# A fused convolution, GELU and two-matmul kernel: first token blocks over two DMA rings, W_in in halves copied across in SBUF, last block stored group by group

## Chip, cores and metric

The kernel runs on one core of one Trainium2 chip. The metric is device time in microseconds (us). Before the change the median of the first four runs is 714.08 us (713.27 to 714.69). A profile's span is about 2 us shorter than the device time of the same run.

Names: PE is TensorE, PEld its weight loads, DVE VectorE, ACT ScalarE, POOL GpSimd, SP SyncE; SPq and ACTq are the DMA issues of SP and ScalarE. A "ring" is the queue of DMAs that one of them issues. "Landing" is when a DMA's semaphore reports it.

## The reference, cut to what matters

```python
w = softmax(weight)                    # 8 heads x 7 taps
# x: 8 x 4096 x 192; causal 7-tap convolution along the sequence, taps per head
out = einsum('hk,bskhg->bshg', w, x_unf)
x = out.reshape(32768, 192)
h = x @ w_in                           # 192 x 2048
g = 0.5 * h * (1.0 + erf(h / sqrt(2))) # exact GELU
return g @ w_out                       # 2048 x 192
```

## The kernel before

The tokens are two halves of 16384, one half on partitions 0 to 63 and the other on 64 to 127, so that two 64-row matmuls share the array. They are cut into 33 blocks per half: two of 256 tokens, then 31 of 512. For each block VectorE transposes and convolves (3 transposes, 21 tap operations), TensorE multiplies by W_in in slices (mm1), ScalarE applies Gelu, and TensorE multiplies by W_out (mm2) during mm1 of the next block. VectorE evicts the result in groups of 128 tokens of each half.

W_in is needed in bf16 on both halves of the partitions. GpSimd loads it with a cast: the first FC = 512 columns twice, once for each half; the other 1536 columns once, and SP then copies them from partitions 0-63 to 64-127 in SBUF.

```python
# GpSimd
g.wait_ge(S_XIN[0], 64)                       # x block 0 has landed
for hf in range(2):
    g.dma_start(win[half hf, columns 0:FC], w_in[..., 0:FC]).then_inc(S_WIN[0], 16)
halo(0)
g.wait_ge(S_XIN[1], 64)                       # x block 1 has landed
g.dma_start(win[half 0, FC:F], w_in[..., FC:F]).then_inc(S_WIN[1], 16)
g.dma_start(wout, w_out).then_inc(S_WOUT, 16)
for n in range(1, NB): halo(n)
# SP
load(0)                                       # 4 DMAs per block
sp.wait_ge(S_XIN[0], 64)
load(1)
sp.wait_ge(S_WIN[1], 16)
sp.dma_start(win[half 1, FC:F], win[half 0, FC:F]).then_inc(S_WIN[2], 16)
load(2)
for n in range(1, NB + 1):
    if n + 2 < NB: load(n + 2)
    store(n - 1)                              # waits for all groups of the block
# TensorE, ahead of mm1 of a block / of the first slice past column FC
t.wait_ge(S_CV, NCV * (n + 1))                # the block's convolution
t.wait_ge(S_WIN[1], 16); t.wait_ge(S_WIN[2], 16)
# ... (cut, in simplified notation)
```

## Time and profile before

| Read from | Before |
|---|---|
| span; TensorE busy | 711.7 us; 95% |
| x block 2 landed; VectorE's wait for it | 34.9; 9.06 us |
| TensorE starts block 2 | 50.66 |
| TensorE's last stretch ends (start of the last eviction) | 706.05 |
| last eviction's start to the end of the span | 5.65 us |

The first fence is the timeline of the kernel before. Columns: start, length (both us), engine, source line, operation, output<-input, count; in brackets how long the engine had been idle just before, and what ended that. A line can merge several instructions, with gaps between them.

```profile
...
0.82 7.07 SPq L434 DMA_DIRECT2D xin<-in_x_dram  x8
...
6.26 1.10 DVE L215 STREAM_TRANSPOSE xT<-xin 128x256 f32<-128x256 f32 x3 [0.74 <-DMA xin<-in_x_dram]
...
13.81 0.63 POOL L178 DMA_DIRECT2D win<-in_moe_w_in_dram  x1 [5.28 <-DMA xin<-in_x_dram]
...
16.44 2.74 PE L361 MATMUL hp<-xc,win 64*128 64x256 bf16 x24 [11.14 <-DVE xc L245]
...
20.10 0.70 SPq L482 DMA_DIRECT2D win<-win  x1
...
27.72 6.04 PE L361 MATMUL hp<-xc,win 64*128 64x256 bf16 x60 [8.54 <-DMA win<-win]
...
34.91 1.90 DVE L215 STREAM_TRANSPOSE xT<-xin 128x512 f32<-128x512 f32 x3 [9.06 <-DMA xin<-in_x_dram]
...
```

VectorE starts at 6.26, and waits 9.06 us for x block 2 at 34.91. TensorE waits 8.54 us for the SBUF copy (`win<-win`) at 27.72. Only one of these waits ends last. The next fence is the chain of waits of the same kernel, in order of time: start, length, and what the next step waited for.

```profile
...
7.46 6.07 DMA xin<-in_x_dram
...
13.81 6.27 DMA win<-in_moe_w_in_dram
20.10 0.70 SPq L482
...
23.82 11.07 DMA xin<-in_x_dram
...
50.66 1.47 PE hp L361 x6
...
```

It runs through x block 1, W_in, x block 2, its convolution and then TensorE's block 2. W_in is in it because SP waits for W_in to issue the copy (20.10), and issues x block 2 only behind that. TensorE's wait for the copy is not in it: TensorE, had it had the data, would have waited for the convolution anyway. From 50.66 the chain is TensorE's to the last eviction.

Why do the loads take until 34.9? This fence is the table of stretches (stretch and length in us; busy time and count of PE, PEld, DVE, ACT, POOL; granted TensorE clock; mean busy share of the 16 DMA engines; GB/s).

```profile
...
4.00:5.00 1.00, 1.00 (x6) 1.00 (x6) 0.00 (x0) 0.43 (x1) 0.00 (x0) 1.00 0.96 229
5.00:6.00 1.00, 0.30 (x2) 0.20 (x1) 0.18 (x1) 0.00 (x0) 0.00 (x0) 1.00 0.01 0
6.00:7.00 1.00, 0.00 (x0) 0.00 (x0) 0.74 (x3) 0.00 (x0) 0.54 (x1) 1.00 0.00 0
12.00:13.00 1.00, 0.00 (x0) 0.00 (x0) 1.00 (x3) 0.00 (x0) 0.00 (x0) 1.00 0.42 61
13.00:14.00 1.00, 0.00 (x0) 0.00 (x0) 1.00 (x4) 0.00 (x0) 0.19 (x1) 1.00 0.09 14
14.00:15.00 1.00, 0.00 (x0) 0.00 (x0) 1.00 (x3) 0.00 (x0) 1.00 (x2) 1.00 0.00 0
...
```

Twice the engines have next to nothing to do: each next load waits until the one before it has been reported as landed. And the same table at the start of block 2 shows the clock:

```profile
...
50.00:51.00 1.00, 0.34 (x2) 0.16 (x4) 1.00 (x3) 0.00 (x0) 0.00 (x0) 0.55 0.00 0
...
53.00:54.00 1.00, 1.00 (x15) 0.64 (x13) 0.96 (x2) 0.31 (x2) 0.69 (x2) 0.75 0.13 27
54.00:55.00 1.00, 1.00 (x21) 0.64 (x18) 1.00 (x4) 1.00 (x2) 0.32 (x1) 1.00 0.48 113
...
```

TensorE had been idle for 3.67 us before block 2 and starts it at half clock (0.55 in the first of these stretches), which lasts until about 53.5 (0.75 is the mean of a stretch half at each). A caution on this column: where the trace has no clock record it reads 1.00, and the first record stands at 19.37 here. So the 1.00 of the first stretches says nothing. The end of the timeline:

```profile
...
696.08 12.69 SPq L461 DMA_DIRECT2D out_dram<-osb  x8
...
706.05 0.56 DVE L254 COPY osb<-ob 128x384 f32<-128x384 f32 x1 [0.76 <-PE ob L393]
```

The last four of these eight stores (192 KB each, the whole last block) are issued only after the last eviction, from 706.6 on.

### The profile page before, as it was taken

Reading aid. Unit: us, or ns where it says so; the run is one execution under the profiler, and the core shown is the slowest. Engines: PE = TensorE matmul, PEld = TensorE weight load, DVE = VectorE, ACT = ScalarE, POOL = GpSimd, SP = SyncE. Lnnn points to the kernel's source line nnn. Section 1 sums busy time; section 2 is a strip of 40 time slices with the busy share of each in tenths; the row PEclk is TensorE's granted clock in tenths of the full one; section 3 lists DMA queues with packets and bytes.
Section 4 is the critical chain, followed back from the end, with each engine's and each line's share of the span. In section 5 each row is a group of like instructions: output and inputs, shape, how many; then the busy total and the mean of one; then the engine's idle time right before and its main releaser. Section 6 shows DMA issues by size and latency. Waiting matters only on the chain.

```text
span 711.7 us, 24838 instructions
## 1 busy us (share of the span) xinstructions
PE 677.3 (95%) x11366; PEld 511.9 (72%) x11366; DVE 563.4 (79%) x925; ACT 526.4 (74%) x516; POOL 37.4 (5%) x77
## 2 busy tenths in 40 slices
PE   1479999999999999999999999999999999999996
PEld 1366777777777777777777777777777777777776
DVE  6499898888889888889888888988888898888701
ACT  1459777777777777777777777777777777777770
POOL 3001000000000000000000000000000000000000
PEclk9799999999999999999999999999999999999999
DMA  6925455544455654345554434555444555543013
GB/s 129 214 57 119 101 134 135 129 104 92 91 122 134 134 122 100 86 97 134 134 134 110 99 84 111 134 134 128 106 95 91 120 134 134 127 96 86 9 44 91
DMA packets 20553, 78.92 MB, mean 111 GB/s; under 512 B 6496, under 2 KB 7904, under 8 KB 16480
## 3 DMA queue, kind: packets, MB, share of 16 engines
q1 hardware_dynamic: 17744, 75.56, 46.9%
q0 software_dynamic: 2688, 1.77, 1.9%
q8 instruction: 89, 1.46, 0.9%
q14 instruction: 16, 0.13, 0.1%
q10 hardware_dynamic: 16, 0.00, 0.0%
HBM read 53.33 MB, written 25.17 MB: 110 GB/s over the span
## 4 chain that ended last, share of the span: by engine, by line
PE 92%; DMA 4%; DVE 2%; SPq 1%; issue 0%
PE ob L393 47%; PE hp L361 45%; DMA xin<-in_x_dram 3%; DVE acc L245 1%; DMA win<-in_moe_w_in_dram 1%; SPq L434 1%; DVE acc L238 0%; DVE xT L215 0%; DVE xc L245 0%; SPq L482 0%; DVE osb L254 0%
## 5 line engine op out<-in xcount | busy, mean ns | idle before, releaser
L321 ACT ACTIVATE gT<-hp 128x1024 bf16<-128x1024 f32 x512 | 523.5, 1024 | 167.9 <-PE hp L361 167.9
L361 PE MATMUL hp<-xc,win 64*128 64x512 bf16 (+1 forms) x3168 | 425.5, 374 | 24.8 <-DVE xc L245 14.8
L393 PEld LDWEIGHTS ob<-wout,gT 64*128 64x128 bf16 x8192 | 364.4, 94 | 107.3 <-issue 0.5
L393 PE MATMUL ob<-wout,gT 64*128 64x192 bf16 x8192 | 426.5, 243 | 0.0
L245 DVE SCALAR_TENSOR_TENSOR acc<-xT,wcol,acc 128x512 f32<-128x512 f32 (+1 forms) x495 | 326.6, 720 | 0.0
L361 PEld LDWEIGHTS hp<-xc,win 64*128 64x128 bf16 x3168 | 159.2, 95 | 82.8 <-issue 26.1
L254 DVE COPY osb<-ob 128x384 f32<-128x384 f32 x128 | 69.9, 546 | 127.6 <-PE ob L393 127.6
L215 DVE STREAM_TRANSPOSE xT<-xin 128x512 f32<-128x512 f32 (+1 forms) x99 | 60.7, 664 | 9.8 <-DMA xin<-in_x_dram 9.8
L245 DVE SCALAR_TENSOR_TENSOR xc<-xT,wcol,acc 128x512 bf16<-128x512 f32 (+1 forms) x99 | 66.4, 718 | 0.0
L238 DVE TENSOR_SCALAR acc<-xT,wcol 128x512 f32<-128x512 f32 (+1 forms) x99 | 57.5, 632 | 1.2
L164 POOL COPY xT<-xT 128x558 f32<-128x558 f32 x33 | 21.6, 653 | 609.2 <-DVE xT L215 609.2
L155 POOL COPY xT<-xT 128x18 f32<-128x18 f32 x29 | 12.1, 419 | 0.0
L332 PE MATMUL ob<-wnm,sel 8*128 8x7 f32 x6 | 1.4, 354 | 3.9 <-DVE wnm L200 3.9
L332 PEld LDWEIGHTS ob<-wnm,sel 8*128 8x128 f32 x6 | 1.3, 320 | 3.9 <-issue 3.9
L298 ACT ACT_TABLE_LOAD x1 | 1.3, 1283 | 1.4 <-PEq L506 1.4
L192 DVE TENSOR_REDUCE wmx<-wsb 8x1 f32<-8x7 f32 x1 | 0.1, 149 | 2.2 <-DMA wsb<-in_weight_dram 2.2
L171 POOL DMA_DIRECT2D win<-in_moe_w_in_dram x2 | 1.4, 686 | 4.0 <-DMA xin<-in_x_dram 4.0
L204 DVE COPY wcol<-ob 128x21 f32<-128x21 f32 x1 | 0.2, 181 | 1.6 <-PE ob L332 1.6
L321 ACT ACT_TABLE_LOAD x1 | 1.3, 1283 | 0.0
L182 POOL DMA_DIRECT2D wout<-in_moe_w_out_dram x1 | 1.2, 1192 | 0.0
L178 POOL DMA_DIRECT2D win<-in_moe_w_in_dram x1 | 0.6, 632 | 5.3 <-DMA xin<-in_x_dram 5.3
L152 POOL MEMSET xT<- 128x18 f32 x4 | 0.8, 206 | 0.0
(12 smaller groups left out, 2.9 us busy)
## 6 DMA issues: line engine op xcount, KB each, us to landing
xin<-in_x_dram SPq DMA_DIRECT2D x124, 380.0 KB, 7.1
out_dram<-osb SPq DMA_DIRECT2D x124, 192.0 KB, 3.1
xin<-in_x_dram SPq DMA_DIRECT2D x8, 188.0 KB, 3.6
wout<-in_moe_w_out_dram POOLq DMA_DIRECT2D x1, 768.0 KB, 10.5
out_dram<-osb SPq DMA_DIRECT2D x16, 48.0 KB, 1.7
win<-in_moe_w_in_dram POOLq DMA_DIRECT2D x1, 576.0 KB, 6.3
win<-win SPq DMA_DIRECT2D x1, 576.0 KB, 7.5
win<-in_moe_w_in_dram POOLq DMA_DIRECT2D x2, 192.0 KB, 6.3
```

Of the source, the lines that this page charges most:

```text
L155: g.tensor_copy(dst, ap(xT[(n - 1) % 2], WS[n - 1] + 31, [[NP * XW, 128], [XW, NP], [32, HB]],),).then_inc(S_HALO)
L164: g.tensor_copy(ap(xT[n % 2], 1, [[NP * XW, 128], [XW, NP], [32, HB], [1, 31]]), ap(xT[n % 2], WS[n], [[NP * XW, 128], [XW, NP], [32, HB], ...
L171: g.dma_start(ap(win, 64 * hf * NP * F, [[NP * F, 64], [F, NP], [1, FC]]), ap(wint, 0, [[F, 64], [64 * F, NP], [1, FC]]),).then_inc(S_WIN[ ...
L215: v.transpose(ap(xT[n % 2], p * XW + HL, [[NP * XW, 128], [1, w]]), ap(xin[n % NX], 64 * p, [[TB // 32 * D, 128], [D, w // 32], [1, 32]],) ...
L238: ins = v.tensor_scalar(a, src, wk, None, ALU.mult)
L245: ins = v.scalar_tensor_tensor(dst, src, wk, a, op0=ALU.mult, op1=ALU.add)
L254: v.tensor_copy(ap(osb[m % 2], g * C, [[8 * C, 128], [4 * C, 2], [1, C]]), ap(ob[(G0[m] + g) % 2], 0, [[1024, 128], [512, 2], [1, C]]),).t ...
L321: a.activation(out=ap(gT[n % 2], i * c * 2 * w, dst), in_=ap(hp[u % 2], 0, src), func=AF.Gelu,).then_inc(S_GELU)
L332: ins = t.matmul(ob[0][:, p * KS : (p + 1) * KS], sel[:, p * 128 : (p + 1) * 128], wnm[:, :],)
L361: ins = t.matmul(hp[u % 2][:, hf * TB + cc * w : hf * TB + cc * w + w], win[r, p * F + f0 : p * F + f0 + 128], xc[n % 2][r, p * TB : p * T ...
L393: ins = t.matmul(ob[gg % 2][:, 512 * sub : 512 * sub + C], gT[m % 2][r, c0 : c0 + 128], wout[r, i * C : (i + 1) * C], start=(ph == 0 and i ...
L434: sp.dma_start(ap(xin[n % NX], 32 * q * (TB // 32 * D), [[TB // 32 * D, 32], [1, mb * D - 32]],), ap(xt, off, [[mb * D, 32], [1, mb * D - ...
```

## The change

Its intent: get the first blocks of x and W_in in sooner, and have less left to store after the last eviction. Blocks 0 and 1 of x are issued by SP and ScalarE, two DMAs of each block, without waiting for each other. W_in's loads wait for nothing; FC is 256; the other columns are loaded in two pieces, one to each half of the partitions, and an SBUF copy carries each across. The last block is stored group by group on both rings, for which its Gelu writes another token order.

```diff
-        FC = 512
+        FC = 256
+        FM = (FC + F) // 2
 # GpSimd
-            g.wait_ge(S_XIN[0], 64)
             for hf in range(2):
                 g.dma_start(... columns 0:FC ...).then_inc(S_WIN[0], 16)
-            halo(0)
-            g.wait_ge(S_XIN[1], 64)
-            g.dma_start(... half 0, FC:F ...).then_inc(S_WIN[1], 16)
+            for hf, c0, c1 in ((0, FC, FM), (1, FM, F)):
+                g.dma_start(... half hf, c0:c1 ...).then_inc(S_WIN[1], 16)
             g.dma_start(... wout ...)
-            for n in range(1, NB):
+            for n in range(NB):
                 halo(n)
 # ScalarE
-            a.dma_start(wsb[:, :], ...)
+            load(a, 0, (2, 3))
             a.wait_ge(S_PRO, 1); a.activation(... Exp ...)
+            load(a, 1, (2, 3))
 # ...
+            for g in range(NG[NB - 1]):
+                store_group(a, NB - 1, g, (2, 3))
 # SP
-            load(0)
-            sp.wait_ge(S_XIN[0], 64)
-            load(1)
-            sp.wait_ge(S_WIN[1], 16)
-            sp.dma_start(... half 1 <- half 0, FC:F ...).then_inc(S_WIN[2], 16)
-            load(2)
+            sp.dma_start(wsb[:, :], ...)
+            load(sp, 0, (0, 1))
+            load(sp, 1, (0, 1))
+            sp.wait_ge(S_WIN[1], 32)
+            for hf, c0, c1 in ((1, FC, FM), (0, FM, F)):
+                sp.dma_start(... half hf <- half 1 - hf, c0:c1 ...).then_inc(S_WIN[2], 16)
+            load(sp, 2)
 # ...
+            for g in range(NG[NB - 1]):
+                store_group(sp, NB - 1, g, (0, 1))
```
(cut: the store helpers and the semaphore counts)

More of the change, by code (lines that the diff above doesn't have):

```diff
@@ L58, in bass_lightweight_conv__then__act_gelu_exact_kernel @@
     G0 = [sum(NG[:n]) for n in range(NB + 1)]
+    PLAIN = [NCH[n] > 1 or n == NB - 1 for n in range(NB)]
     OUTS = []
     for n in range(NB):
-        OUTS.append((64 if NCH[n] == 1 else 128) + (OUTS[n - 2] if n >= 2 else 0))
+        OUTS.append((64 * NG[n] if PLAIN[n] else 64) + (OUTS[n - 2] if n >= 2 else 0))
     es = ExitStack()
@@ L118, in bass_lightweight_conv__then__act_gelu_exact_kernel, with load, store_group, store @@
         NCV = NP * KS
-        FC = 512
+        FC = 256
+        FM = (FC + F) // 2
+        def load(e, n, qs=(0, 1, 2, 3)):
+            mb = WS[n] // 32
+            if n >= NX:
+                e.wait_ge(S_TR, NP * (n - NX + 1))
+            for q in qs:
+                off = ((q // 2) * HALF + OFF[n]) * D + 32 * (q % 2)
+                e.dma_start(
+                    ap(
+                        xin[n % NX],
+                        32 * q * (TB // 32 * D),
+                        [[TB // 32 * D, 32], [1, mb * D - 32]],
+                    ),
+                    ap(xt, off, [[mb * D, 32], [1, mb * D - 32]]),
+                ).then_inc(S_XIN[n % NX], 16)
+        def store_group(e, m, g, qs=(0, 1, 2, 3)):
+            mb = WS[m] // 32
+            e.wait_ge(S_EV, G0[m] + g + 1)
+            for q in qs:
+                e.dma_start(
+                    ap(
+                        outt,
+                        (OFF[m] + 4 * g + q) * C,
+                        [[mb * C, 32], [HALF * C, 2], [1, C]],
+                    ),
+                    ap(
+                        osb[m % 2],
+                        32 * q * 8 * C + g * C,
+                        [[8 * C, 32], [4 * C, 2], [1, C]],
+                    ),
+                ).then_inc(S_OUT[m % 2], 16)
+        def store(e, m):
+            if PLAIN[m]:
+                for g in range(NG[m]):
+                    store_group(e, m, g)
+                return
+            j = NG[m]
+            mb = WS[m] // 32
+            e.wait_ge(S_EV, G0[m + 1])
+            for q in range(4):
+                e.dma_start(
+                    ap(
+                        outt,
+                        (OFF[m] + j * q) * C,
+                        [[mb * C, 32], [HALF * C, 2], [1, j * C]],
+                    ),
+                    ap(
+                        osb[m % 2],
+                        32 * q * 8 * C,
+                        [[8 * C, 32], [4 * C, 2], [1, j * C]],
+                    ),
+                ).then_inc(S_OUT[m % 2], 16)
         @block.gpsimd
@@ L174, in _ @@
                 ).then_inc(S_WIN[0], 16)
-            halo(0)
-            g.wait_ge(S_XIN[1], 64)
-            g.dma_start(
-                ap(win, FC, [[NP * F, 64], [F, NP], [1, F - FC]]),
-                ap(wint, FC, [[F, 64], [64 * F, NP], [1, F - FC]]),
-            ).then_inc(S_WIN[1], 16)
+            for hf, c0, c1 in ((0, FC, FM), (1, FM, F)):
+                g.dma_start(
+                    ap(win, 64 * hf * NP * F + c0, [[NP * F, 64], [F, NP], [1, c1 - c0]]),
+                    ap(wint, c0, [[F, 64], [64 * F, NP], [1, c1 - c0]]),
+                ).then_inc(S_WIN[1], 16)
             g.dma_start(
@@ L295, in _ @@
         def _(a):
-            a.dma_start(wsb[:, :], ap(wt, 0, [[KS, H], [1, KS]])).then_inc(S_WSB, 16)
+            load(a, 0, (2, 3))
             a.wait_ge(S_PRO, 1)
@@ L312, in _ @@
                         a.wait_ge(S_MM2, G0[n - 1])
-                    if c == 1:
+                    if not PLAIN[n]:
                         src = [[2 * TB, 128], [w // 4, 8], [32, w // 128], [1, 32]]
@@ L352, in mm1 @@
                 if seen[0] == 1 and 128 * (i + 1) * c > FC:
-                    t.wait_ge(S_WIN[1], 16)
-                    t.wait_ge(S_WIN[2], 16)
+                    t.wait_ge(S_WIN[1], 32)
+                    t.wait_ge(S_WIN[2], 32)
                     seen[0] = 2
@@ L427, in _ @@
         def _(sp):
-            def load(n):
-                mb = WS[n] // 32
-                if n >= NX:
-                    sp.wait_ge(S_TR, NP * (n - NX + 1))
-                for q in range(4):
-                    off = ((q // 2) * HALF + OFF[n]) * D + 32 * (q % 2)
-                    sp.dma_start(
-                        ap(
-                            xin[n % NX],
-                            32 * q * (TB // 32 * D),
-                            [[TB // 32 * D, 32], [1, mb * D - 32]],
-                        ),
-                        ap(xt, off, [[mb * D, 32], [1, mb * D - 32]]),
-                    ).then_inc(S_XIN[n % NX], 16)
@@ L443, in store @@
-            def store(m):
-                w = WS[m]
-                j = w // 128
-                mb = w // 32
-                sp.wait_ge(S_EV, G0[m + 1])
-                for q in range(4):
-                    if NCH[m] == 1:
-                        dst = ap(
-                            outt,
-                            (OFF[m] + j * q) * C,
-                            [[mb * C, 32], [HALF * C, 2], [1, j * C]],
-                        )
-                        src = ap(
-                            osb[m % 2],
-                            32 * q * 8 * C,
-                            [[8 * C, 32], [4 * C, 2], [1, j * C]],
-                        )
-                        sp.dma_start(dst, src).then_inc(S_OUT[m % 2], 16)
-                    else:
-                        assert j == 2
-                        for b in range(2):
-                            dst = ap(
-                                outt,
-                                (OFF[m] + 4 * b + q) * C,
-                                [[mb * C, 32], [HALF * C, 2], [1, C]],
-                            )
-                            src = ap(
-                                osb[m % 2],
-                                32 * q * 8 * C + b * C,
-                                [[8 * C, 32], [4 * C, 2], [1, C]],
-                            )
-                            sp.dma_start(dst, src).then_inc(S_OUT[m % 2], 16)
@@ L478, in _ @@
-            load(0)
-            sp.wait_ge(S_XIN[0], 64)
-            load(1)
-            sp.wait_ge(S_WIN[1], 16)
-            sp.dma_start(
-                ap(win, 64 * NP * F + FC, [[NP * F, 64], [F, NP], [1, F - FC]]),
-                ap(win, FC, [[NP * F, 64], [F, NP], [1, F - FC]]),
-            ).then_inc(S_WIN[2], 16)
-            load(2)
-            for n in range(1, NB + 1):
+            sp.dma_start(wsb[:, :], ap(wt, 0, [[KS, H], [1, KS]])).then_inc(S_WSB, 16)
+            load(sp, 0, (0, 1))
@@ L488, in _ @@
+            load(sp, 1, (0, 1))
+            sp.wait_ge(S_WIN[1], 32)
+            for hf, c0, c1 in ((1, FC, FM), (0, FM, F)):
+                sp.dma_start(
+                    ap(win, 64 * hf * NP * F + c0, [[NP * F, 64], [F, NP], [1, c1 - c0]]),
+                    ap(win, 64 * (1 - hf) * NP * F + c0, [[NP * F, 64], [F, NP], [1, c1 - c0]]),
+                ).then_inc(S_WIN[2], 16)
+            load(sp, 2)
+            for n in range(1, NB):
                 if n + 2 < NB:
-                    load(n + 2)
@@ L490, in _ @@
-                store(n - 1)
+                    load(sp, n + 2)
+                store(sp, n - 1)
+            for g in range(NG[NB - 1]):
+                store_group(sp, NB - 1, g, (0, 1))
             for s in range(2):
```

## The prediction

> **What bounds it now.** From 50.7 us on, the chain of waits is TensorE alone: 31 blocks of about 20.8 us, ending at 706.0 (busy summary: PE 95% of a 711.7 us span). The change touches nothing there; at most the first 50.7 us and the last 5.7 us can shrink.
>
> Head, from the chain of waits and the timeline: x block 0 lands 6.16; block 1 is issued only then and lands 13.5; the rest of W_in is issued only then (13.81) and lands 20.08; the SBUF copy is issued 20.10 and lands 27.7; x block 2, behind it in the SP ring, lands 34.9. VectorE convolves blocks 0 and 1 without a break from 6.26 to 25.85, then waits 9.06 us for x block 2; its convolution takes 15.6 us, and TensorE starts block 2 at 50.66. TensorE also waits 8.5 us for the W_in copy (19.2 to 27.7), but is done with that work at 47.0, so that wait is hidden behind block 2's convolution by 3.7 us.
>
> Tail: last eviction ends 706.61; SP issues four 192 KB stores (706.6 to 708.7); data moves until 711.0; landed about 711.3.
>
> **What the change does.** Second ring: the x loads already run the DMA engines at a share of 0.87 to 0.98 (2 to 5 us), with SP issuing one per 0.46 us. The Trainium skill ("DMA: Bandwidth & Descriptors", "Issuing engines are not separate DMA queues") says that issuing from several engines saves only issue time; the trace agrees, so I give the second ring itself nearly nothing in the head. What helps is the removed waits: DMA engines idle about 2.0 us (5 to 7) and 2.5 us (12.4 to 15), by the windows table. These 4.5 us go. Bytes to move until x block 2 is in: W_in reads fall 0.2 MB, the copy grows 0.1 MB: nearly even. So x block 2, still last in the queue, lands about 5 us earlier: near 30 (estimate; 27.5 to 32), not at 25.9 where VectorE is ready.
>
> - VectorE start: about 6 to 6.5, no gain (the softmax weights are ready only at 5.5, and ScalarE now issues two loads before its Exp). Not critical: VectorE still waits about 4 us for x block 2 (was 9.06).
> - W_in: first part about 9, halves about 14.7, copies about 22.5 (7.6 us copy as before, beside W_out). With FC 256 only one slice of block 0 runs before it; seven remain. From copy to end of block 1's work: 19.3 us before, one slice (1.3 us) more now: TensorE ready at about 43.
> - Block 2's convolution: 30 + 15.6, TensorE starts block 2 at about 45.7 instead of 50.66: **4.9 us**.
> - Tail: only the last group (4 stores of 48 KB, two per ring) remains after 706.6: second issue at about 707.1, plus 1.7 us (landing of such stores in the issue table): 708.8 instead of 711.3: **2.5 us**.
> - Last block's other Gelu layout: both forms take 1.02 us: 0.
>
> **Prediction:** 714.1 - 4.9 - 2.5 = **706.7 us**, range 702.8 to 710. Faster by over 2%: 0.02; within 2%: 0.97; slower by over 2%: 0.01.
>
> **Right if** VectorE's wait before block 2's transposes shrinks from 9.1 to about 4 us and still ends with x block 2; TensorE starts block 2 near 45.7; the block period stays 20.8; last matmul to end of span falls from 5.7 to about 3.2.
>
> **Wrong if** the W_in copies, and x block 2 behind them, come sooner (engines used better by mixed traffic): up to 4 us more, capped by VectorE's 25.9 + 15.6; or later, if W_out's 768-byte rows or the two rings hold them up; if TensorE, with the W_in copies late, becomes the last to arrive at block 2; or if 768-byte store rows land slowly.

## The result, and the profile after

The changed kernel takes 704.2 us (median of 4 runs, 703.88 to 704.52) against 714.08. The ratio is 0.9862, 95% interval 0.9845 to 0.9879. A ratio here is the mean time of one kernel's runs over that of the other's of the same rounds, so not quite the ratio of the quoted medians. The gain of 9.9 us is clear of the noise.

| | Before | After | Predicted |
|---|---|---|---|
| x block 2 landed | 34.9 | 28.1 | about 30 |
| VectorE's wait for it | 9.06 us | 2.87 us | about 4 us |
| TensorE starts block 2 | 50.66 | 43.83 | about 45.7 |
| from there to the last eviction's start | 655.39 us | 654.82 us | unchanged |
| last eviction's start to end of span | 5.65 us | 3.35 us | about 3.2 us after the last matmul |
| span | 711.7 us | 702.0 us | |

The three parts give 6.83 + 0.57 + 2.30 = 9.70 us, the whole difference of the spans. First the timeline after:

```profile
...
6.09 1.10 DVE L273 STREAM_TRANSPOSE xT<-xin 128x256 f32<-128x256 f32 x3 [0.28 <-DMA xin<-in_x_dram]
...
13.29 1.35 SPq L495 DMA_DIRECT2D win<-win  x2
...
14.68 5.35 SPq L130 DMA_DIRECT2D xin<-in_x_dram  x8
...
15.80 1.46 PE L423 MATMUL hp<-xc,win 64*128 64x256 bf16 x12 [10.20 <-DVE xc L303]
...
20.95 4.68 PE L423 MATMUL hp<-xc,win 64*128 64x256 bf16 x48 [3.68 <-DMA win<-win]
...
28.08 1.90 DVE L273 STREAM_TRANSPOSE xT<-xin 128x512 f32<-128x512 f32 x3 [2.87 <-DMA xin<-in_x_dram]
...
36.69 0.48 PE L423 MATMUL hp<-xc,win 64*128 64x256 bf16 x5 [1.87 <-issue]
...
43.83 0.82 PE L423 MATMUL hp<-xc,win 64*128 64x512 bf16 x6 [2.05 <-DVE xc L303]
...
```

VectorE still waits for x block 2, so that is still what sets block 2; the wait is 2.87 us instead of 9.06. VectorE's own start at 6.09 has hardly moved. The copies are issued at 13.29 (20.10 before) and TensorE has them at 20.95 (27.72). TensorE waits only 2.05 us before block 2. The line at 36.69 is a pause of 1.87 us in block 1's work that this view gives no reason for ("issue"); before it was 0.93 us. Run e7 comes back to it.

```profile
...
5.00:6.00 1.00, 0.60 (x3) 0.50 (x3) 0.18 (x1) 0.00 (x0) 1.00 (x1) 1.00 0.99 211
6.00:7.00 1.00, 0.00 (x0) 0.00 (x0) 0.91 (x3) 0.00 (x0) 0.32 (x2) 1.00 1.04 266
12.00:13.00 1.00, 0.00 (x0) 0.00 (x0) 1.00 (x4) 0.00 (x0) 0.00 (x0) 1.00 1.43 185
...
14.00:15.00 1.00, 0.00 (x0) 0.00 (x0) 1.00 (x4) 0.00 (x0) 0.00 (x0) 1.00 1.61 194
...
```

The same stretches that stood idle before are now full. (The time of each packet is added up, so packets of several queues in flight together give a share above 1.) In half-us stretches, counting what is missing where the share is below a half, idle time from 1 us to the landing of x block 2 is 0.5 us against 5.2 before: 4.7 of the 6.83 us. The rest is not idle time.

```profile
...
43.00:44.00 1.00, 0.17 (x2) 0.14 (x4) 1.00 (x3) 0.00 (x0) 0.00 (x0) 1.00 0.00 0
44.00:45.00 1.00, 1.00 (x16) 0.66 (x14) 1.00 (x3) 0.30 (x1) 0.00 (x0) 1.00 0.00 0
...
```

The clock is 1.00 at the start of block 2. And the end of the timeline:

```profile
...
692.64 7.39 SPq L144 DMA_DIRECT2D out_dram<-osb  x8
692.64 7.45 ACTq L144 DMA_DIRECT2D out_dram<-osb  x8
...
698.65 0.56 DVE L312 COPY osb<-ob 128x384 f32<-128x384 f32 x1 [0.76 <-PE ob L455]
```

Eight stores on each ring now (48 KB each); three quarters of them are issued before the last eviction.

### The profile page after: what moved, and what is told of

Its sections match the earlier page's. It is cut to its first block, busy times and chain, and to the rows that moved or that the text cites. A ratio compares the mean times of both kernels' runs of the same rounds, so it can differ in the third digit from the quotient of the medians.

```text
span 702.0 us, 24852 instructions
## 1 busy us (share of the span) xinstructions
PE 675.1 (96%) x11366; PEld 517.8 (74%) x11366; DVE 563.0 (80%) x925; ACT 526.3 (75%) x516; POOL 37.2 (5%) x78
## 3 DMA queue, kind: packets, MB, share of 16 engines
q8 instruction: 89, 1.46, 0.9%
## 4 chain that ended last, share of the span: by engine, by line
PE 91%; DVE 4%; DMA 3%; SPq 1%; issue 1%; POOL 0%; POOLq 0%
PE ob L455 47%; PE hp L423 44%; DVE acc L303 3%; DMA xin<-in_x_dram 1%; DMA win<-in_moe_w_in_dram 1%; DVE xT L273 0%; DVE xc L303 0%; DVE acc L296 0%; SPq L130 0%; DVE osb L312 0%; POOL win L229 0%; SPq L495 0%; POOL win L236 0%; POOL sel L185 0%; POOL sel L195 0%
## 5 line engine op out<-in xcount | busy, mean ns | idle before, releaser
L455 PEld LDWEIGHTS ob<-wout,gT 64*128 64x128 bf16 x8192 | 369.1, 94 | 101.9
L423 PEld LDWEIGHTS hp<-xc,win 64*128 64x128 bf16 x3168 | 162.9, 95 | 74.6 <-issue 19.2
```

What stands on the lines that cost most here:

```text
L423: ins = t.matmul(hp[u % 2][:, hf * TB + cc * w : hf * TB + cc * w + w], win[r, p * F + f0 : p * F + f0 + 128], xc[n % 2][r, p * TB : p * T ...
L455: ins = t.matmul(ob[gg % 2][:, 512 * sub : 512 * sub + C], gT[m % 2][r, c0 : c0 + 128], wout[r, i * C : (i + 1) * C], start=(ph == 0 and i ...
```

## Experiments

Theory "waits": the loads' waits for one another left the DMA engines idle; taking them away brings x block 2 sooner, and block 2's convolution starts at its landing. Rivals: "ring" (the second ring brings the head's gain), "halves" (W_in in two pieces does). For the tail: group by group, or the second ring.

Medians of before are 714.08, 713.95, 713.88, 714.16 and 713.90, so medians can be set side by side to some 0.3 us. "Start" is TensorE's start of block 2.

| Run | Time us | Ratio to before (95%) | x block 2 | Start |
|---|---|---|---|---|
| after | 704.20 | 0.9862 (0.9845-0.9879) | 28.08 | 43.83 |
| e1_waits_only | 708.56 | 0.9920 (0.9906-0.9933) | 29.55 | 45.31 |
| e2_tail_only | 711.86 | 0.9966 (0.9952-0.9981) | 34.77 | 50.53 |
| e3_one_ring_head | 705.04 | 0.9873 (0.9855-0.9891) | 28.12 | 43.87 |
| e4_one_ring_tail | 704.85 | 0.9869 (0.9854-0.9883) | 27.56 | 43.31 |
| e5_whole_tail | 705.56 | 0.9881 (0.9866-0.9896) | 27.79 | 43.54 |
| e6_x2_first | 706.10 | 0.9889 (0.9875-0.9904) | in time | 46.08 |
| e7_hold_x3 | 705.15 | 0.9871 (0.9855-0.9888) | 27.61 | 43.35 |
| e8_win_waits | 707.68 | 0.9911 (0.9896-0.9926) | 32.12 | 47.88 |
| e9_act_copy | 712.33 | 0.9970 (0.9958-0.9982) | in time | 52.01 |
| e10_act_copy_warm | 713.45 | 0.9987 (0.9975-0.9999) | in time | 54.13 |
| e11_hold_warm | 703.25 | 0.9848 (0.9836-0.9861) | 27.28 | 42.94 |
| e12_act_copy_order | 701.52 | 0.9825 (0.9812-0.9839) | in time | 41.17 |

"In time": VectorE did not wait for it. All were correct.

### e1: only the waits taken away

```diff
 # on the kernel before
-            g.wait_ge(S_XIN[0], 64)
...
-            halo(0)
-            g.wait_ge(S_XIN[1], 64)
...
-            sp.wait_ge(S_XIN[0], 64)
```

> The kernel before with nothing changed but the waits in front of x block 1 and of the two parts of W_in taken away (one ring, FC 512, W_in in one piece, one SBUF copy, old tail). Theory 'waits' (the head gain is the removed waits): x block 2 lands near 28 to 29 us and TensorE starts block 2 near 44 to 44.5 (50.66 before, 43.83 after), time about 707 us. Theory 'ring' (the second ring brings the head gain) or theory 'halves' (the split of W_in and of its copy brings it): most of the gain is missing, TensorE starts block 2 after 47 us, time above 710 us.

x block 2 lands at 29.55 and block 2 starts at 45.31: 5.35 of the 6.83 us. So the waits are most of it, but my expected 44 to 44.5 was too early: 1.48 us are missing, nearly all of which e3 assigns. The time, 708.56 us, is also later than my 707. TensorE waited 3.73 us before block 2 and its clock fell to 0.50 from about 46.2 to 49.6, so part of the earlier start was given back.

### e2: only the new tail

```diff
 # on the changed kernel: loads, FC, W_in and the copy as before; the tail stays
```

> The kernel before with only the new tail (last block evicted and stored group by group over two rings, its other Gelu layout). All theories of the head: start of block 2 stays at 50.7. The stores alone should give the whole tail gain: last matmul to end of span 3.4 us instead of 5.7, time about 711.8 us. If the Gelu layout costs anything, the last block's Gelu takes more than 1.02 us and the time is higher.

As expected: 711.86 us; the start stays at 50.5, the last eviction's start to the end takes 3.47 us (5.65 before), and Gelu takes 1.02 us in the last block too.

### e3: first blocks on one ring

```diff
-            load(a, 0, (2, 3))
-            load(a, 1, (2, 3))
-            load(sp, 0, (0, 1))
-            load(sp, 1, (0, 1))
+            load(sp, 0)
+            load(sp, 1)
```

> The changed kernel with all loads of x blocks 0 and 1 on the SP ring. Theory 'waits': the same as the changed kernel, start of block 2 at 43.8 within 0.5 us, time 704.2 within 0.6. Theory 'ring': x blocks land later, W_in copies too, start of block 2 later by 2 us or more, time above 706.

Block 2 starts at 43.87 against 43.83; the profiled run's span is 702.1 against 702.0. VectorE starts at 7.16 instead of 6.09, but only waits less for x block 2 afterwards (1.84 instead of 2.87 us). "Ring" falls for the head. The median, 705.04 (703.79 to 706.69), is 0.24 us over the band I had given; the intervals overlap. Set beside e1, which also has one ring and no waits, e3 differs in the head only by FC and the halves of W_in (and by who loads the small tap weights): x block 2 lands 1.43 us sooner. So "halves", with FC, has its share, about a fifth. FC and the split were not tried apart, and runs whose heads are the same differ by up to 0.5 us (see e7).

### e4 and e5: the tail's two parts

```diff
 # e4: on the changed kernel
-            for g in range(NG[NB - 1]):
-                store_group(a, NB - 1, g, (2, 3))
...
-                store_group(sp, NB - 1, g, (0, 1))
+                store_group(sp, NB - 1, g)
 # e5: on the changed kernel: the last block stored whole on both rings
-    PLAIN = [NCH[n] > 1 or n == NB - 1 for n in range(NB)]
+    PLAIN = [NCH[n] > 1 for n in range(NB)]
...
+            store(a, NB - 1, (2, 3))
...
+            store(sp, NB - 1, (0, 1))
```

> The changed kernel with the last block's group stores all on the SP ring. If group by group is what counts, the second ring saves only two issues of about 0.43 us after the last eviction: last matmul to end of span about 4.2 us instead of 3.4, time about 705.0. If the second ring is what counts, the tail goes back to about 5.7 us, time about 706.5.

> The changed kernel with the last block stored whole (192 KB pieces, after all its evictions) but over two rings. If group by group counts, the 786 KB still move at some 207 GB/s (3.8 us) after the last eviction, the second ring only starts them earlier: last matmul to end of span about 5.0 to 5.7 us instead of 3.4, time about 706. If the second ring counts, it stays near 3.4 us and 704.2.

From the last eviction's start to the end of the span: 5.65 us before, 5.45 with two rings alone (e5), 4.59 with groups alone (e4), 3.35 with both. With whole stores, 786 KB still have to move after the last eviction, and the second ring saves only 0.20 us. With groups the last piece is small, what is left is the issuing, and there the second ring saves 1.24 us, more than the two issues of 0.43 us that I had counted: in e4 SP was still issuing the group before, and issued the last store at 700.71, against 699.65 in the changed kernel. These are single traces; the medians differ by 0.65 us (e4) and 1.36 us (e5), as both heads came out a little sooner (table).

### e6: x block 2 ahead of the copies

```diff
+            load(sp, 2)
             sp.wait_ge(S_WIN[1], 32)
             for hf, c0, c1 in ...: # the two copies
-            load(sp, 2)
```

> The changed kernel with the load of x block 2 issued ahead of the W_in copies in the SP ring. If x block 2 alone sets the start of block 2, it lands near 20 us, VectorE convolves without a break and TensorE starts block 2 near 41, time about 701.5. If TensorE's own chain is close behind (copies near 26 us, plus about 20.8 us for the work of blocks 0 and 1), TensorE starts block 2 near 47 and the time is about 707. I expect the second.

```profile
...
17.53 1.47 PE L423 MATMUL hp<-xc,win 64*128 64x256 bf16 x12 [11.94 <-DMA win<-in_moe_w_in_dram]
...
25.31 1.88 DVE L273 STREAM_TRANSPOSE xT<-xin 128x512 f32<-128x512 f32 x3
...
27.52 4.69 PE L423 MATMUL hp<-xc,win 64*128 64x256 bf16 x48 [8.53 <-DMA win<-win]
...
46.30 0.56 DVE L312 COPY osb<-ob 128x384 f32<-128x384 f32 x1 [4.70 <-PE ob L455]
...
```

This is its timeline. VectorE never waits for x (25.31 has no bracket), but TensorE gets W_in at 17.53 and the copies at 27.52, and is itself the last to arrive at block 2, at 46.08, 2.25 us after the changed kernel. The order "copies, then block 2" is right; the slack of TensorE's chain is the 2.05 us of its wait in the changed kernel, and 3.91 us where the pause in block 1's work is missing (e7). It is missing here too, so copies 6.57 us later cost only 2.25 us.

### e7: block 3 held back

```diff
                 if n + 2 < NB:
+                    if n == 1:
+                        sp.wait_ge(S_XIN[2], 64)
                     load(sp, n + 2)
```

> The changed kernel with the load of x block 3 held until x block 2 has landed. If block 3's transfer takes bandwidth from block 2's, block 2 lands up to 1 us earlier (27.1 instead of 28.1), TensorE starts it near 42.9, time about 703.3. If the ring is strictly first in first out, nothing changes: 28.1, 43.8, 704.2.

x block 2 lands at 27.61; the changed kernel, e4 and e5, whose heads are the same, show 28.08, 27.56 and 27.79. So holding block 3 back does nothing that shows for block 2's landing. Yet the time is 705.15 us, although block 2 starts 0.48 us sooner than in the changed kernel. These are stretches of e7:

```profile
...
41.00:42.00 1.00, 0.00 (x0) 0.00 (x0) 1.00 (x3) 0.00 (x0) 0.00 (x0) 1.00 0.00 0
42.00:43.00 1.00, 0.00 (x0) 0.00 (x0) 1.00 (x2) 0.00 (x0) 0.00 (x0) 0.64 0.00 0
43.00:44.00 1.00, 0.65 (x4) 0.33 (x6) 1.00 (x3) 0.00 (x0) 0.00 (x0) 0.50 0.00 0
...
49.00:50.00 1.00, 1.00 (x17) 0.68 (x15) 1.00 (x3) 0.77 (x2) 0.00 (x0) 0.94 0.44 102
...
```

TensorE had no pause in block 1's work in this run, was done at 39.4, waited 3.91 us, and ran at half clock from 42.3 to 49.1. That is a new theory, tested by e11: TensorE's wait before block 2 decides whether it keeps its full clock there.

The missing pause is hardly chance. In all nine runs that have the pause it comes after TensorE's 221st matmul and ends 1.2 to 1.5 us after a packet of 16 KiB on the DMA queue that the profile calls "instruction" (q8): in the changed kernel the packet moved from 34.02 to 35.26, and TensorE stood from 34.83 to 36.69. In the five runs without it the packet was through more than 5 us before TensorE came to that place; in e7 and e11, which hold block 3 back, it moved already at 27.9, in the gap between the loads of blocks 2 and 3. So TensorE seems to wait there for its instructions, which come late behind block 3's load. This is read from the times of the records; no run moved the packet alone.

### e11: the same with TensorE kept busy in its wait

```diff
 # on e7, TensorE, ahead of its wait for block 2's convolution
+                if n == 2 and i == 0:
+                    for k in range(WARM):            # WARM = 8
+                        for hf in range(2):
+                            t.matmul(hp[u % 2][half hf], win[r, 0:128], win[r, 0:TB],
+                                     start=True, stop=True, ...)  # overwritten by mm1
```

> The changed kernel with block 3's load held back (as in the earlier run, which took 705.15 us at mean clock 0.995) and the same eight pairs of matmuls in TensorE's wait before block 2. If the half clock at the start of block 2 made that run slower than the changed kernel, this one runs the first slices of block 2 at 0.98 us instead of 1.9 us each and takes 703.5 to 704.2 at a mean clock of 0.998 or more. If holding block 3 back made it slower, it stays at 705.

The timeline of e11:

```profile
...
39.33 1.91 PE L414 MATMUL hp<-win 64*128 64x512 bf16 x16
...
42.94 0.82 PE L436 MATMUL hp<-xc,win 64*128 64x512 bf16 x6 [1.71 <-DVE xc L304]
...
43.93 0.81 PE L436 MATMUL hp<-xc,win 64*128 64x512 bf16 x6
...
```

The useless matmuls (`hp<-win`) end at 41.2, and block 2's slices start 0.98 us apart; e7's first were 1.9 us apart. The time is 703.25 us against 705.15 for e7, mean clock 0.998 to 1.000 against 0.995 to 0.997. Within e7, too, the one run at 0.997 took 703.96 us, the three at 0.995 took 705.11 to 705.29. The clock theory holds. Whether e11 beats the changed kernel (704.20) the intervals do not separate.

### e8: W_in's waits put back

```diff
 # on the changed kernel, GpSimd
+            g.wait_ge(S_XIN[0], 64)
             for hf in range(2): # columns 0:FC
...
+            g.wait_ge(S_XIN[1], 64)
             for hf, c0, c1 in ((0, FC, FM), (1, FM, F)):
```

> The changed kernel with the two waits of the W_in loads put back (first part after x block 0 has landed, the rest after x block 1 has landed), all else as changed. If only idle time of the DMA engines counts, these stand idle about 2 us more, and x block 2 lands about 2 us later (30). If in addition the loads run faster when W_in's casting loads and the x loads overlap, it is 3 to 4 us (31 to 32). Start of block 2 near 46 or near 47.5; time about 706.3 or 707.8.

x block 2 lands at 32.12, 4.04 us later, and block 2 starts at 47.88; time 707.68. By half-us stretches the DMA engines stand idle 2.2 us against 0.5, so 1.7 us of the 4 are idle time; the rest is work done more slowly, for nearly the same bytes (5.97 against 5.87 MB by those stretches). This supports, but does not isolate, that the engines do more per us when W_in's loads overlap those of x. One side effect: the first halo copy stands behind the second wait on GpSimd, and VectorE waited 4.6 us for it. That cost nothing here, for VectorE still had to wait 2.54 us for x block 2.

### e9, e10 and e12: the copies on ScalarE

```diff
 # e9: on the changed kernel; SP's two copies and its wait on S_WIN[1] are gone
             load(a, 1, (2, 3))
+            a.wait_ge(S_WIN[1], 32)
+            for hf, c0, c1 in ((1, FC, FM), (0, FM, F)):
+                a.activation(out=win[half hf, c0:c1], in_=win[half 1 - hf, c0:c1],
+                             func=AF.Copy).then_inc(S_WIN[2], 16)
 # e10: e9 with the useless matmuls of e11
 # e12: e10 with
+            sp.wait_ge(S_WIN[1], 32)                    # SP, ahead of load(sp, 2)
+            a.activation(out=dmy, in_=wsb, func=AF.Gelu) # loads Gelu's table early
 #      and WARM = 5
```

> The changed kernel with the two SBUF copies of W_in done by ScalarE (idle then) instead of by DMA. If x block 2 waits for the DMA engines to get through the bytes queued ahead of it, taking 0.69 MB of copies away brings it about 3 us earlier (near 25 instead of 28) and VectorE's wait before it all but goes; TensorE starts block 2 near 41. If then TensorE's own wait before block 2 grows past some 3.5 us, its clock falls to half as in the run that held block 3 back and 1 to 2 us are lost again: time 701.5 with a full clock, 702.5 to 703.5 with the fall. If the order in the ring and not the bytes sets block 2's landing, it comes only with the time saved on the issue, and the time stays at 704.

> The same with eight pairs of matmuls without use (64x512, results overwritten) in TensorE's wait before block 2. If the clock theory holds, the clock stays at 1.00 through the start of block 2, and the time is 701.5 or just below. If the fall of the clock costs nothing, no difference to the run without them.

Both went wrong, by my edit: with the copies SP had also lost its wait for W_in, so x blocks 2 and 3 were issued right away. The timeline of e9:

```profile
...
7.26 2.38 SPq L130 DMA_DIRECT2D xin<-in_x_dram  x4
...
24.24 1.46 PE L430 MATMUL hp<-xc,win 64*128 64x256 bf16 x12 [18.66 <-DMA win<-in_moe_w_in_dram]
...
27.04 4.91 ACT L366 ACTIVATE win<-win 64x2688 bf16<-64x2688 bf16 x2 [23.63 <-DMA win<-in_moe_w_in_dram]
...
```

W_in's first part reaches TensorE at 24.24 and the rest ScalarE at 27.04, against 15.8 at the latest and 13.3 in the changed kernel. With some 4.5 MB of x queued on the rings (four DMAs of 188 KB for each of blocks 0 and 1, four of 380 KB for each of blocks 2 and 3), W_in was nearly the last to land. So one wait of the changed kernel earns its keep: SP's, which holds x block 2 back until W_in is in. The useless matmuls of e10 could only delay TensorE, which was the late one. Neither says anything on the clock.

> The ScalarE copies again, but with SP still waiting for W_in to land before it issues x block 2 (the first try had lost that wait, and x blocks 2 and 3 then went ahead of W_in), with Gelu's table loaded before the copies and five pairs of useless matmuls in TensorE's wait before block 2. If the bytes queued ahead set x block 2's landing: W_in lands near 13.3 as in the changed kernel, x block 2 near 25 (28.1 there), VectorE goes through without a long wait, TensorE starts block 2 near 41.2 at full clock, time 701.6. If x block 2 still lands near 28 us, the bytes of the copies were not what it waited for, and the time is 704.

With the order kept it works. The timeline of e12:

```profile
...
13.68 4.91 ACT L369 ACTIVATE win<-win 64x2688 bf16<-64x2688 bf16 x2 [8.75 <-DMA win<-in_moe_w_in_dram]
...
18.74 4.98 PE L445 MATMUL hp<-xc,win 64*128 64x256 bf16 x48 [1.09 <-ACT win L369]
...
25.52 1.88 DVE L275 STREAM_TRANSPOSE xT<-xin 128x512 f32<-128x512 f32 x3
...
41.17 0.82 PE L445 MATMUL hp<-xc,win 64*128 64x512 bf16 x6 [1.57 <-DVE xc L305]
...
```

ScalarE copies from 13.68 to 18.59, TensorE has the columns at 18.74 (20.95 with the DMA copies), and x block 2 is there before VectorE wants it (25.52 has no bracket; its semaphore reports it at 25.07, against 28.06 in the changed kernel). So x block 2 does wait behind the 0.69 MB of copies queued ahead of it: without them it lands 3.0 us sooner, and its first DMA is issued only 1.07 us sooner (13.61 against 14.68). Block 2 starts at 41.17, and the time is 701.52 us (701.41 to 701.72), faster than before and after the change, with intervals apart. From its start at 6.48 VectorE now convolves blocks 0 to 2 without a wait for data from DMA; that is the head's new limit. How much of the step from e9 to e12 is due to the early table load, or to the useless matmuls, was not tried.

## Why the prediction was right

- **Overall: right, a little cautious.** 706.7 predicted, 704.2 measured, within 702.8 to 710. The mechanism held: waits out of the loads, x block 2 sooner, block 2's convolution with it, nothing from the second ring there (e1, e3).
- **The mis-sized term: x block 2 "about 5 us earlier"**, counted from idle time alone. Both inputs held: 4.5 us of idle time were to go, 4.7 went, and the bytes moved until x block 2 is in were nearly even (5.98 MB before, 5.89 after). Yet x block 2 came 6.83 us sooner: the busy engines got through the same bytes 2.1 us faster. My "Wrong if" had named this (engines used better by mixed traffic), the sum had not. Removing the waits alone brought block 2's start forward by 5.35 us (e1), against 4.9 predicted for the whole head; the halves with FC bring 1.43 us more (e1 against e3).
- **"The change touches nothing there"**, of TensorE's work from block 2 on, was wrong by 0.57 us, the balance of two things. TensorE's wait before block 2 shrank from 3.67 to 2.05 us and it no longer started at half clock: the first two slices of block 2 took 0.98 us each instead of 1.88 and 1.46, a gain of 1.38 us. But then it waits for block 3's convolution, which costs 0.81 us (its first slice, at 60.28, starts 1.79 us after the one before it, not 0.98). I had seen the wait before block 2 and not the clock beside it. That the clock costs time at this place is shown by e7 and e11 (1.9 us there). That the changed kernel kept its clock was luck: the pause in block 1's work, which nobody had planned, shortened the wait, and without the pause e7 lost the clock.
- **The W_in chain: "halves about 14.7, copies about 22.5", TensorE "ready at about 43"**: measured 13.3, 20.9 and 41.8. All somewhat too late, as with x block 2.
- **Tail: "2.5 us"**: 2.30 measured; e2 alone gives 2.18. That both parts are needed was not in the prediction: groups without the ring give 1.06 us, the ring without groups 0.20 us.
- **Gelu's other layout, 0**: right, 1.02 us.
- **The skill.** "DMA: Bandwidth & Descriptors", section "Issuing engines are not separate DMA queues", says that several issuing engines save only the issue time. The runs agree twice: in the head the second ring changes block 2's start by 0.04 us (e3), and in the tail, where little but issuing remains, it is worth 1.24 us (e4). "TensorE: Matmul & The Clock Gate", Part 1, says that the clock falls to half after an idle window of about 3.4 us that runs free of the program. Here waits before block 2 of 3.35 (e2), 3.67 (before), 3.73 (e1) and 3.91 us (e7) came with half clock, waits of 2.98 (e8), 2.05 (after) and 1.71 us (e11) did not.

Still open: FC against the split of W_in; whether TensorE's pause in block 1's work (0.93 us before, 1.87 after, none in e7) is a wait for instructions, as the times suggest; and why the loads run faster when they overlap.

## What to carry to other kernels

Where loads at the start wait for one another, look at the share of the DMA engines in those stretches: idle time there is most of the gain (4.7 of 6.83 us here), and a second ring brought nothing; but keep the wait that stops a large, later load from going ahead of a small, urgent one, and take bytes off the queue where an idle engine can do the move. At the end, cut the last store small first; only then is it worth issuing from two rings. Before removing part of an idle time of TensorE, read its granted clock after it, and check it by the spacing of the slices.

## What the Trainium skill lacked or had wrong

- "DMA: Bandwidth & Descriptors", "Queues, rings and completion order", says that a DMA engine goes round robin between queues, packet by packet. It doesn't say how bytes divide when GpSimd's casting loads of short rows meet long x rows: in e9 W_in's first 0.2 MB (as bf16) reached TensorE at 24.24 us, beside some 4.5 MB of x on the other queues, of which block 2 had landed at 16.82 and block 3 landed at 24.51.
- "TensorE: Matmul & The Clock Gate", Part 1, gives the window as an idle one. It doesn't say how much work a window may hold and still count as idle. In every trace here the recorded changes of the clock lie multiples of 3.41 us apart. In the windows of 3.41 us so marked off, TensorE was idle for 2.00 us or more in each of the 20 that ended with a fall, and for at most 1.99 us (the changed kernel, at block 2) in each one at full clock that did not; the ends of matmuls are modelled, so the line between is not that sharp. So the place of a wait counts beside its length: 2.98 us lay across two windows without a fall (e8). And the fall can come after work has begun again: in e1 TensorE waited 3.73 us, 2.56 of them in the window that ended at 46.16, started block 2 at 45.31 at full clock, and had half clock from 46.2 to 49.6.
- "Runtime: NRT & Kernel Launch", section "Instruction fetch mechanics", says that fetching instructions in blocks of 16 KiB is mostly hidden. It doesn't say that queued loads can delay a block, nor how to see it. TensorE pauses once in block 1's work, for 0.74 us (e12) to 1.87 us (after), where the timeline shows it waiting for nothing, each time until 1.2 to 1.5 us after a 16 KiB packet of the "instruction" queue (see e7). That the one waits for the other is likely from these times, and not shown by a run of its own.
